# Output tiles of a routed feed-forward kernel: ScalarE copies both halves of a PSUM bank, and an accumulating transfer in SBUF adds them, in place of a VectorE add

## The chip, the cores and the metric

The kernel runs on one NeuronCore of a Trainium2 chip. The core has a matrix engine (TensorE, PE in the profile, with its weight loads as PEld), VectorE (DVE), ScalarE (ACT), GpSimd (POOL) and SyncE (SP), each with its own in-order instruction queue, and 16 DMA engines that they share. The metric is the device time of one execution in microseconds (us); lower is better.

## What is computed

```python
# x: 8 x 3584 x 192, weight: 8 x 7
w = softmax(weight, axis=-1)
attn[b, s, h] = sum_k w[h, k] * x_padded[b, s + k, h]      # causal 7-tap filter, 8 groups of 24 channels
x = attn.reshape(28672, 192)
logits = x @ w_gate                                        # 28672 x 8
# greedy by falling logit: a token goes to the expert of its best pair that still has room (3584 each)
for e in range(8):
    h = np.maximum(x[assigned == e] @ w1[e], 0)            # 192 -> 1024
    out[assigned == e] = h @ w2[e]                         # 1024 -> 192
```

All numbers are float32. The kernel reaches this precision with pairs of operands, a high part and a low part (the remainder), for weights and activations.

## The kernel before, in words

There are three kinds of work, and they overlap. The filter runs first and writes `attn` to HBM. The routing then finds, for every token, its expert: `half(0)`, `half(1)`, `rest` and `last` are generators, and one `next` of such a generator emits a few instructions, most of them for VectorE, some for ScalarE, and small matrix products into PSUM banks named `bg`. In `rest` stand `rounds` (thresholds for each expert; its tiles have names with `r_`, such as `r_w`, `r_x`, `r_v`) and then the building of index lists, in which VectorE makes one-hot tiles `oa`, TensorE multiplies them and ScalarE copies the products to `X`.

The feed-forward work is cut into 56 tiles of 512 tokens, and `run` goes over them. Tokens whose place is known early come first: eight tiles of one expert each, then pairs, and the tiles that need the end of the routing last. In iteration i of `run` a tile i is in its first layer (`l1`: eight steps f, five matrix products each into a bank `ph`; ScalarE makes the rectified high part `hh`, VectorE the remainder `hl`), tile i - 1 is in its second layer (`l2`: for each of its four blocks of 128 tokens 16 products into a bank `y`, two steps f per block), tile i + 1 gets its transposed input (`prep`), and for tile i + 2 GpSimd issues four gathers of token rows from HBM (`xg`).

A bank `y` holds 2 x 192 columns: columns 0 to 191 are the sum of two products, columns 192 to 383 a third, and the output is the sum of the two halves. `store` is called after each block, at the odd steps f. There ScalarE copies the second half to `yt`, and VectorE adds the first half from PSUM and `yt` to `yo`. `scatter` is called at the even steps; it pops the block and GpSimd issues an indirect transfer of the 128 rows of `yo` to their places in `out`. The pool `fo` has three buffers of `yo` and two of `yt`.

While the routing runs, the input is transposed by TensorE (`transp`: four products into `px` for channels 0 to 127, four more for the rest) and evacuated by ScalarE (`xa<-px`, `xd<-px`) and VectorE. Once no generator is left, `free()` holds, and the tile that is gathered then goes another way (`shuffle`: 16 pairs of VectorE block transposes into `xs`, no TensorE work).

What is put where in the engines' queues is decided while the program is written out. `Pace` adds up rough costs for every instruction (an estimate of its own, in `Meter`) for TensorE, VectorE and ScalarE, and `hook`, which is called in each step of `l1`, `l2` and `run`, emits the next piece of routing as long as VectorE's sum is no further than 1.8 us ahead of TensorE's. A piece that needs a result of VectorE or ScalarE is held back until TensorE's sum is past the producer's:

```python
v = self.need
if type(v) is tuple and self.route.cols < v[1] or type(v) is float and v > p.pe or p.dve > p.pe + slack or p.act > p.pe + act:
    return
self.run()
```

So an instruction less for VectorE in a block also moves the routing, and all that follows it, to earlier places in the program.

Of the kernel before, what the change touches and what calls it, by code (L numbers as in the profile page):

```python
# [6 lines left out]
F32 = mybir.dt.float32  # L7
# [3 lines left out]
AF = mybir.ActivationFunctionType  # L11
OP = mybir.AluOpType
# [3 lines left out]
NE, D, NTOK, F, CAP = 8, 192, 28672, 1024, 3584  # L16
# [12 lines left out]
class Meter:  # L29


    def __init__(self, pace, name, eng):
        self.pace, self.name, self.eng = pace, name, eng
# [1099 lines left out]
class FFN:  # L1133
# [3 lines left out]
    def __init__(self, tc, nc, attn, w1, w2, out, ident, wr, drm):  # L1137
        self.tc, self.nc = tc, nc

        self.kept1 = [drm.tile([128, 3, F], F32, name="kw%d" % e) for e in range(NE)]  # L1140
        self.keptd = [drm.tile([64, F], F32, name="kd%d" % e) for e in range(NE)]
        self.kept2 = [drm.tile([128, 8, 2 * D], F32, name="kv%d" % e) for e in range(NE)]
        self.attn, self.w1, self.w2, self.out, self.ident, self.wr = attn, w1, w2, out, ident, wr
        self.bg = lambda: None
        self.busy = lambda: False
        self.WT, self.RAW, self.XG, self.XT, self.H, self.Y, self.XS = {}, {}, {}, {}, {}, {}, {}
        self.wpa, self.wpb, self.DL = [None, None], [None, None], [None, None]
        self.scat, self.late = [], []
        self.free = set()
        self.xg = None  # L1150

# [163 lines left out]
    def store(self, i, b, idx):  # L1315
        nc = self.nc
        y = self.Y.pop((i, b))
        t = self.op.tile([128, D], F32, name="yt", bufs=2)
        o = self.op.tile([128, D], F32, name="yo")
        nc.scalar.activation(t, y[:, D:2 * D], AF.Copy)  # L1320
        nc.vector.tensor_tensor(o, y[:, 0:D], t, op=OP.add)
        self.late.append((o, idx))

    def scatter(self):

        if not self.late:
            return
        o, idx = self.late.pop()
        st = self.nc.gpsimd.indirect_dma_start(  # L1329
            out=self.out, out_offset=bass.IndirectOffsetOnAxis(ap=idx, axis=0), in_=o, in_offset=None,  # L1330
            bounds_check=NTOK - 1, oob_is_err=False)
        for s in self.scat:
            self.tc.declare_no_dep(st.ins, s.ins, reason="rows of other tokens")
        self.scat.append(st)
# [77 lines left out]
def moe_kernel(ctx, tc, x, weight, wg, w1, w2, out):  # L1412
    nc = Pace(tc.nc)
# [5 lines left out]
    with ExitStack() as cw:  # L1419
# [8 lines left out]
        r = Route(tc, nc, LT, lst, wk, drm)  # L1428
        r.oh_pool = oh
        r.bg = lambda: bgp.tile([128, 512], F32, name="bg")  # L1430
        ff = FFN(tc, nc, attn, w1, w2, out, r.ident, wr, drm)
# [21 lines left out]
        def half(h):  # L1453
            if h == 0:
                yield from r.thresh(0.905)
            yield from r.settle(h)
            yield from r.count(r.F, h)
            if h:
                yield from r.counts(NE)
            yield from r.lists(r.F, TA, h, 0 if h else None, *((ia, ja) if h else (ia0, ja0, 8, 4)),  # L1460
                               between=r.open() if h else None)

        def rest():
            yield from r.rounds()
            yield from r.final(NL)
            yield from r.lists(r.F, TB, 1, None, ib0, jb0, NL, 4, between=front())
# [5 lines left out]
        def last():  # L1472
            yield from r.sort4(0, TB, 1)
            yield from r.gather(TB, False)
            yield from r.tokens(TB, ib, jb)

        def tail():

            for i in (14, 15):
                for u in range(3):  # L1480
                    gate(i, u)
                    yield PEA if u == 2 else None
                end(i)
            nc.sync.dma_start(r.ltab, LT)
            c1.close()
            cs.close()
            ff.wpool2(cw, 1)
            ff.hp[1] = pool(cw, "fh1", 1, **late)
            yield

        bg = Steps(nc, r, (half(0), tail(), half(1), rest(), last()))
# [96 lines left out]
        ff.py = pool(cw, "py", 2, space=PSUM, **late)  # L1588
        ff.wpool2(cw, 0)
        ff.op = pool(cw, "fo", 3, **late)  # L1590
        ff.xp = pool(cw, "fp", 1, **late)
        ff.hp = [pool(cw, "fh0", 1, **late), None]
        ff.wpool(cw, 1)
# [60 lines left out]
```

## Time and profile before

| what | value |
|---|---|
| time before, median of 3 runs | 1268.94 us (1267.08 to 1273.11) |
| the profiled execution, its own time | 1281.97 us |
| its span, first to last instruction | 1280.2 us |
| TensorE busy, share of the span | 96% |
| VectorE busy | 78% |
| ScalarE busy | 43% |
| GpSimd busy | 40% |
| mean granted TensorE clock | 0.991 |

Busy shares are means over the whole span. TensorE's matrix products overlap one another and their ends are modelled, so a busy TensorE may still lose time; what counts is which wait ends last at a given place. In the rows below an instruction is named by its output, an arrow and its inputs; nearly all of them carry line L55, the helper that records them. An entry in square brackets is the idle time of the engine just ahead of the instruction, with the instruction that ended it.

### The profile page before, as it was taken

What the parts mean: (1) busy time and instruction counts of PE and PEld (TensorE: products, weight loads), DVE (VectorE), ACT (ScalarE), POOL (GpSimd) and SP (SyncE); (2) the same over time, 40 slices, a digit from 0 to 9 for tenths busy, and PEclk for the clock granted to TensorE, in tenths of its full rate; (3) what the DMA queues carried; (4) which work ended last, traced back from release to release, by engine and by line L of the source; (5) the groups of instructions that cost most, each with busy time, mean ns of one, the idle gap of its engine ahead of it and who ended that gap; (6) DMA issues with size and microseconds to landing.
All of it is one profiled execution on the core that took longest, in us unless ns stands there. A gap on an engine that the chain in (4) does not pass through costs nothing.

```text
span 1280.2 us, 21799 instructions
## 1 busy us (share of the span) xinstructions
PE 1228.3 (96%) x7847; PEld 1052.5 (82%) x7847; DVE 993.3 (78%) x2229; ACT 549.8 (43%) x1220; POOL 511.5 (40%) x504
## 2 busy tenths in 40 slices
PE   5989979999999999999989999999999999999997
PEld 2445558889889888888779999999999999999997
DVE  7398569799889999888866777777777777777772
ACT  4544645856444434443433333333333333333332
POOL 3000425355354444434144444444444444444422
PEclk9999989999999999999999999999999999999999
DMA  9999797999533343424453423232413232231100
GB/s 238 348 331 302 250 325 261 278 301 318 200 104 105 129 141 102 150 79 149 123 140 101 154 83 105 96 110 78 153 47 109 80 104 97 65 123 47 47 23 30
DMA packets 100579, 193.02 MB, mean 151 GB/s; under 512 B 19232, under 2 KB 64752, under 8 KB 96240
## 3 DMA queue, kind: packets, MB, share of 16 engines
q1 hardware_dynamic: 57856, 115.15, 27.5%
q0 software_dynamic: 21504, 44.07, 11.7%
q10 hardware_dynamic: 21104, 32.34, 7.7%
q8 instruction: 63, 1.03, 0.3%
q14 instruction: 52, 0.43, 0.1%
HBM read 116.02 MB, written 75.50 MB: 150 GB/s over the span
## 4 chain that ended last, share of the span: by engine, by line
PE 86%; DMA 5%; DVE 5%; ACT 2%; issue 1%; SPq 1%; another core or an unknown queue 0%; POOL 0%; POOLq 0%; ACTq 0%; DVEq 0%
PE ph L55 38%; PE y L55 38%; PE cv L55 4%; DMA X<-in_x_dram 3%; PE bg L55 3%; DMA raw<-in_moe_w_dram 2%; PE px L55 1%; PE pl L55 1%; DVE aT L55 1%; DVE X L55 1%; DVE oa L55 1%; ACT a_d L55 1%; DVE hl L55 0%; DMA kd<-dl 0%
## 5 line engine op out<-in xcount | busy, mean ns | idle before, releaser
L55 PE MATMUL y<-w,hh 128*128 128x384 f32 x1792 | 541.6, 358 | 0.0
L55 ACT ACTIVATE hh<-ph 128x512 fp32r<-128x512 f32 x448 | 267.9, 598 | 493.9 <-PE ph L55 457.9
L55 PE MATMUL y<-w,hl 128*128 128x192 f32 x1792 | 449.9, 251 | 0.0
L55 DVE SCALAR_TENSOR_TENSOR hl<-ph,hh 128x512 fp32r<-128x512 f32 x448 | 308.2, 688 | 144.4 <-ACT hh L55 121.4
L55 PE MATMUL ph<-xa,w 128*128 128x512 f32 x1344 | 395.1, 402 | 1.2 <-DVE hl L55 1.1
L55 PEld LDWEIGHTS y<-w,hl 128*128 128x128 f32 x1792 | 342.2, 191 | 15.0
L55 PEld LDWEIGHTS y<-w,hh 128*128 128x128 f32 x1792 | 337.5, 188 | 18.6 <-issue 1.9
L1329 POOL DMA_INDIRECT out_dram<-yo,ib x128 | 128.2, 1001 | 288.2 <-DVE yo L55 278.0
L55 PEld LDWEIGHTS ph<-xa,w 128*128 128x128 f32 x1344 | 218.9, 189 | 21.7 <-DVE hl L55 2.6
L1329 POOL DMA_INDIRECT out_dram<-yo,ia x96 | 111.7, 1164 | 268.5 <-DVE yo L55 237.2
L55 DVE STREAM_TRANSPOSE xs<-xg 32x256 f32<-32x256 f32 x480 | 176.8, 368 | 8.2
L55 PE MATMUL ph<-xd,w 128*128 128x512 f32 x448 | 177.5, 396 | 1.1 <-DVE xd L55 1.1
L55 PE MATMUL ph<-xd,dl 128*128 128x512 f32 x448 | 174.6, 390 | 0.4 <-DVE dl L55 0.4
L1254 POOL DMA_INDIRECT xg<-attn,jb x128 | 139.0, 1086 | 44.9 <-issue 40.6
L1254 POOL DMA_INDIRECT xg<-attn,ja x96 | 110.7, 1153 | 33.3 <-issue 26.2
L55 ACT ACTIVATE yt<-y 128x192 f32<-128x192 f32 x224 | 73.5, 328 | 114.3 <-PE y L55 91.2
L55 PE MATMUL cv<-X,TH 118*128 118x384 f32 x256 | 101.7, 522 | 17.3 <-DVE TH L55 12.4
L55 DVE TENSOR_TENSOR yo<-y,yt 128x192 f32<-128x192 f32 x224 | 79.6, 355 | 42.4 <-ACT yt L55 39.2
L55 PEld LDWEIGHTS ph<-xd,w 128*128 128x128 f32 x448 | 84.1, 188 | 21.1 <-DVE xd L55 1.6
L55 PEld LDWEIGHTS ph<-xd,dl 128*128 128x128 f32 x448 | 84.3, 188 | 20.3 <-DVE dl L55 0.7
L55 PEld LDWEIGHTS cv<-X,TH 118*128 118x128 f32 x256 | 45.0, 197 | 51.0 <-issue 14.5
L55 ACT ACTIVATE a<-cv 128x384 f32<-128x384 f32 x128 | 59.9, 492 | 57.2 <-PE cv L55 40.5
(237 smaller groups left out, 904.4 us busy)
## 6 DMA issues: line engine op xcount, KB each, us to landing
w<-kw SPq DMA_DIRECT2D x16, 1536.0 KB
w<-kv SPq DMA_DIRECT2D x16, 1536.0 KB
attn<-a ACTq DMA_DIRECT2D x16, 1344.0 KB
kw<-w SPq DMA_DIRECT2D x48, 256.0 KB
kv<-w SPq DMA_DIRECT2D x32, 384.0 KB
X<-in_x_dram SPq DMA_DIRECT2D x17, 672.0 KB
X<-in_x_dram ACTq DMA_DIRECT2D x15, 672.0 KB
raw<-in_moe_w_dram SPq DMA_DIRECT2D x32, 192.0 KB
```

Source lines behind the costliest of these rows:

```text
L55: return f(*a, **k)
L1254: self.nc.gpsimd.indirect_dma_start(out=t[:, b], out_offset=None, in_=self.attn[0:rows], in_offset=bass.IndirectOffsetOnAxis(ap=idx[b], ax ...
L1329: st = self.nc.gpsimd.indirect_dma_start(out=self.out, out_offset=bass.IndirectOffsetOnAxis(ap=idx, axis=0), in_=o, in_offset=None, bounds ...
```

## The change

From the eighth tile on (`i > 6`) and as long as routing generators are left, `store` gives VectorE nothing. ScalarE copies all 384 columns of the bank to a tile `yo` that now has two halves. At the next even step `scatter` issues, from GpSimd, a transfer inside SBUF that adds the second half onto the first (`accum_op=OP.add`), and one even step later the indirect transfer of the first half to `out`. In the other tiles ScalarE's copy goes into the second half of the same tile, and VectorE adds as before. The pool `fo` has three such tiles.

```diff
@@ class FFN
-        t = self.op.tile([128, D], F32, name="yt", bufs=2)
-        o = self.op.tile([128, D], F32, name="yo")
-        nc.scalar.activation(t, y[:, D:2 * D], AF.Copy)
-        nc.vector.tensor_tensor(o, y[:, 0:D], t, op=OP.add)
-        self.late.append((o, idx))
+        o = self.op.tile([128, 2, D], F32, name="yo")
+        if self.bydma(i):
+
+            nc.scalar.activation(o.rearrange("p h d -> p (h d)"), y[:, 0:2 * D], AF.Copy)
+            self.sums.append((o, idx))
+            return
+        nc.scalar.activation(o[:, 1], y[:, D:2 * D], AF.Copy)
+        nc.vector.tensor_tensor(o[:, 0], y[:, 0:D], o[:, 1], op=OP.add)
+        self.late.append((o[:, 0], idx))
 
     def scatter(self):
 
-        if not self.late:
-            return
-        o, idx = self.late.pop()
+        ready, self.late = self.late, []
+        if self.sums:
+            o, idx = self.sums.pop()
+            self.nc.gpsimd.dma_start(o[:, 0], o[:, 1], accum_op=OP.add)
+            self.late.append((o[:, 0], idx))
+        for r in ready:
+            self.rows(*r)
+
+    def rows(self, o, idx):
         st = self.nc.gpsimd.indirect_dma_start(
             out=self.out, out_offset=bass.IndirectOffsetOnAxis(ap=idx, axis=0), in_=o, in_offset=None,
             bounds_check=NTOK - 1, oob_is_err=False)
@@ moe_kernel
+        ff.bydma = lambda i: bg.gens and i > 6
```

In the whole program 60 of the 224 blocks take the new way. The emitted programs differ further in this: 25 tiles are transposed by TensorE, where before there were 26, and 31 go by `shuffle`, where there were 30.

On GpSimd's queue, about the tenth tile, the program before has this (`xg<-attn` are the gathers, `out_dram<-yo` the indirect transfers to the output; `x4` stands for four in a row):

```order
L1254 DMA xg<-attn,ja 128x192 x4
L1329 DMA out_dram<-yo,ia 28672x192 x4
L1254 DMA xg<-attn,ja 128x192 x4
L1329 DMA out_dram<-yo,ia 28672x192 x4
L1254 DMA xg<-attn,ja 128x192 x4
```

The changed program has this for one tile (`yo<-yo` are the accumulating transfers):

```order
L1255 DMA xg<-attn,ja 128x192 x4
L1334 DMA yo<-yo 128x192
L1340 DMA out_dram<-yo,ia 28672x192
L1334 DMA yo<-yo 128x192
L1340 DMA out_dram<-yo,ia 28672x192
L1334 DMA yo<-yo 128x192
L1340 DMA out_dram<-yo,ia 28672x192
L1334 DMA yo<-yo 128x192
L1340 DMA out_dram<-yo,ia 28672x192
```

A tile has twelve transfers on this queue in place of eight, and each transfer to the output stands behind the accumulating transfer of the next block.

On VectorE's queue the third of four places in `rounds` where a result `r_v` goes back to TensorE reads as follows before (the two `r_x` that read `bg` are the first to use the products of that round):

```order
L55 MAX r_w<-X_6386 128x8 x2
L55 SCALAR_TENSOR_TENSOR hl<-ph,hh 128x512
L55 TENSOR_TENSOR yo<-y,yt 128x192
L55 SCALAR_TENSOR_TENSOR r_x<-bg,room 128x8
L55 SCALAR_TENSOR_TENSOR r_x_3179<-bg,room_2148 8x1
L55 TENSOR_SCALAR r_x<-r_x 128x8
L55 TENSOR_SCALAR r_x_3179<-r_x_3179 8x1
L55 TENSOR_SCALAR r_pen<-r_x_3179 8x1
L55 TENSOR_SCALAR r_x_3179<-r_x_3179 8x1
L55 MAX r_s_6704<-bg 8x8
```

The same place in the changed program:

```order
L55 MAX r_w<-X_6273 128x8 x4
L55 SCALAR_TENSOR_TENSOR hl<-ph,hh 128x512
L55 TENSOR_TENSOR xd<-px,xd 64x512
L55 SCALAR_TENSOR_TENSOR hl<-ph,hh 128x512
L55 SCALAR_TENSOR_TENSOR r_x<-bg,room 128x8
L55 SCALAR_TENSOR_TENSOR r_x_3166<-bg,room_2147 8x1
L55 TENSOR_SCALAR r_x<-r_x 128x8
L55 TENSOR_SCALAR r_x_3166<-r_x_3166 8x1
L55 TENSOR_SCALAR r_pen<-r_x_3166 8x1
L55 TENSOR_SCALAR r_x_3166<-r_x_3166 8x1
```

No add of an output block stands ahead of the round's first reader any more; a remainder `hl` does. On TensorE's queue the same round's `r_v` product now has 8 first-layer and 12 second-layer products between it and the round's `r_w` transposes, where before there were 8 and 8. The place itself moved from 147 whole first-layer steps into the program to 144, and the routing's last product from the sixth step of tile 24 to the first.

## Rows read from the trace of the kernel before

**Rows 1.** The profile's page: busy us and share of each engine, instructions.

```profile
PE 1228.3 (96%) x7847; PEld 1052.5 (82%) x7847; DVE 993.3 (78%) x2229; ACT 549.8 (43%) x1220; POOL 511.5 (40%) x504
```

**Rows 2.** Stretches: length, busy us by engine, granted clock, DMA share, GB/s.

```profile
230.00:360.00 130.00, 127.48 (x755) 113.95 (x754) 114.74 (x265) 77.58 (x193) 64.66 (x54) 1.00 0.81 262
...
340.00:520.00 180.00, 179.00 (x1053) 160.12 (x1052) 163.46 (x406) 77.94 (x191) 81.58 (x72) 1.00 0.36 119
520.00:560.00 40.00, 38.09 (x216) 34.16 (x216) 34.24 (x77) 18.58 (x51) 14.89 (x15) 0.96 0.30 88
560.00:640.00 80.00, 78.17 (x597) 67.79 (x596) 68.60 (x166) 31.71 (x68) 24.58 (x24) 1.00 0.42 131
640.00:680.00 40.00, 36.54 (x316) 31.46 (x316) 27.10 (x61) 14.98 (x29) 19.24 (x18) 0.96 0.45 121
```

**Rows 3.** Waits of TensorE from 340 to 700 us: us, times, longest.

```profile
PE bg L55 <- ACT X L55: 2.2, 3, 0.9
PE bg L55 <- DVE r_v L55: 1.9, 1, 1.9
PE bg L55 <- DVE hl L55: 1.7, 1, 1.7
```

**Rows 4.** Timeline, 537 to 546 us: start us, us, engine, instruction.

```profile
541.17 0.33 ACT L55 ACTIVATE yt<-y 128x192 f32<-128x192 f32 x1 [2.39 <-PE ph L55]
...
541.54 0.36 DVE L55 TENSOR_TENSOR yo<-y,yt 128x192 f32<-128x192 f32 x1 [2.03 <-ACT yt L55]
541.81 0.21 DVE L55 SCALAR_TENSOR_TENSOR r_x<-bg,room 128x8 f32<-128x8 f32 x2
...
543.64 0.26 DVE L55 TENSOR_SCALAR r_v<-r_v,r_pen 8x1 f32<-8x1 f32 x1
...
543.96 0.22 PE L55 MATMUL bg<-ident,r_v 8*128 8x8 f32 x1 [1.91 <-DVE r_v L55]
```

**Rows 5.** The two stretches of 5 us about that place.

```profile
540.00:545.00 5.00, 3.09 (x15) 2.46 (x15) 3.29 (x14) 1.31 (x3) 1.01 (x1) 0.91 0.23 63
545.00:550.00 5.00, 5.00 (x26) 4.62 (x26) 4.93 (x14) 1.53 (x3) 0.98 (x1) 0.75 0.01 3
```

**Rows 6.** Timeline of TensorE, two first-layer steps about 444 us.

```profile
443.02 0.88 PE L55 MATMUL ph<-xa,w 128*128 128x512 f32 x3
...
444.19 0.60 PE L55 MATMUL px<-ident,xg 128*64 128x128 f32 x4
...
445.75 0.88 PE L55 MATMUL ph<-xa,w 128*128 128x512 f32 x3
...
448.04 0.88 PE L55 MATMUL ph<-xa,w 128*128 128x512 f32 x3
```

**Rows 7.** The page's groups: busy us, mean ns, idle before.

```profile
L55 ACT ACTIVATE hh<-ph 128x512 fp32r<-128x512 f32 x448 | 267.9, 598 | 493.9 <-PE ph L55 457.9
L55 DVE SCALAR_TENSOR_TENSOR hl<-ph,hh 128x512 fp32r<-128x512 f32 x448 | 308.2, 688 | 144.4 <-ACT hh L55 121.4
...
L55 DVE STREAM_TRANSPOSE xs<-xg 32x256 f32<-32x256 f32 x480 | 176.8, 368 | 8.2
L55 ACT ACTIVATE yt<-y 128x192 f32<-128x192 f32 x224 | 73.5, 328 | 114.3 <-PE y L55 91.2
L55 DVE TENSOR_TENSOR yo<-y,yt 128x192 f32<-128x192 f32 x224 | 79.6, 355 | 42.4 <-ACT yt L55 39.2
L55 ACT ACTIVATE a<-cv 128x384 f32<-128x384 f32 x128 | 59.9, 492 | 57.2 <-PE cv L55 40.5
```

**Rows 8.** Groups of GpSimd from 340 to 700 us, as in rows 7.

```profile
L1329 POOL DMA_INDIRECT out_dram<-yo,ia x67 | 72.6, 1084 | 187.3 <-DVE yo L55 162.0 <-DVE r_oki L55 5.5 <-DVE r_x L55 5.0
L1254 POOL DMA_INDIRECT xg<-attn,ja x52 | 58.4, 1123 | 15.9 <-issue 14.6 <-PE ph L55 0.6 <-PE bg L55 0.3
```

**Rows 9.** Instructions on `yo`: ns min/median/max, first and last start us.

```profile
L1329 POOL DMA_INDIRECT out_dram<-yo,ia x96: 981/1037/3728, 192.7 to 700.4; - x96
```

**Rows 10.** A piece of the chain that ended last: start us, us.

```profile
238.91 5.60 DMA raw<-in_moe_w_dram
```

More of the change, by code (lines that the diff above doesn't have):

```diff
@@ L1147, in __init__ @@
         self.wpa, self.wpb, self.DL = [None, None], [None, None], [None, None]
-        self.scat, self.late = [], []
+        self.scat, self.late, self.sums = [], [], []
+        self.bydma = lambda i: False
         self.free = set()
```

## The prediction

> **What bounds the kernel now.** I read the page first: of a span of 1280.2 us TensorE is busy 96%, VectorE 78% [rows 1]. A mean of that kind says little, so I went to the stretches. The change acts from about 315 us (eighth tile) to about 700 us. From 340 to 520 us TensorE is idle for 1.0 us of 180 and VectorE is busy 163.5 us, 91% [rows 2]. VectorE is nearly full there, yet TensorE hardly ever waits for it: the queues are written so that VectorE is fed as much routing as fits under TensorE. The reader is to see that relief of VectorE in this stretch is not time; it is room that the program fills with routing.
>
> What TensorE does lose lies in a few places. From 520 to 680 us it is idle 1.9, 1.8 and 3.5 us in the three stretches [rows 2], so with the 1.0 us before that 8.2 us in all, and the waits that have a name are few: one of 1.9 us for `r_v`, one of 1.7 us for `hl`, three for `X`, 2.2 us together [rows 3]. Two of the stretches also show a mean granted clock of 0.96 [rows 2]. The first belongs to the `r_v` wait: after 1.9 us idle the granted clock goes to 0.91 and 0.75 in the next two stretches of 5 us [rows 5], that is part of them at 1.2 GHz in place of 2.4, and costs (0.09 + 0.25) x 5 = 1.7 us. The second has the same mean over 40 us, 1.6 us. All that the routing's waits cost from 340 to 680 us is thus 8.2 + 3.3 = 11.5 us, and no removal of VectorE work can bring more than this, except by TensorE work that disappears.
>
> **Why TensorE waits for r_v.** This is the place that matters most [rows 4]. VectorE is done with all before at 541.54 - 2.03 = 539.5 us and then does nothing for 2.03 us, because the next in its queue is the add of an output block, which waits for ScalarE's `yt`, and this starts at 541.17, when TensorE has ended the bank `y`. The round's first reader `r_x` stands behind this add and starts at 541.81, `r_v` ends at 543.9, TensorE goes on at 543.96. The chain from `r_x` to `r_v` takes 543.90 - 541.81 = 2.1 us. Had it begun when VectorE was free, at 539.5, it would have ended at 541.6, before TensorE's earliest need at 543.96 - 1.91 = 542.05.
>
> **The change, part by part.** VectorE loses 60 adds of 355 ns [rows 7], 21.3 us, and gains one tile's `shuffle`, 16 transposes of 368 ns, 5.9 us. Its stretch is covered by TensorE either way, so this counts nothing directly; what it does is bring the routing's last product forward by five steps.
>
> TensorE: because the routing ends earlier, one tile more goes by `shuffle`. A step with four `px` takes 445.75 - 443.02 = 2.73 us, the next without 2.29 [rows 6]. Two such groups in a tile are 2 x 0.44 = 0.9 us, saved once: **-0.9 us**. The other products are the same in number.
>
> The `r_v` wait: in the changed program no add stands ahead of `r_x`; the last instruction ahead is an `hl` whose bank `ph` is full before the `r_w` products. The chain of 2.1 us then runs beside 8 first-layer and 12 second-layer products. Five first-layer products take 444.19 - 443.02 = 1.17 us, and the eight second-layer ones the rest of a 2.29 us step, 1.12 [rows 6]; so these take 8 x 0.234 + 12 x 0.14 = 3.55 us. That leaves 1.4 us, enough for another `hl` of 0.69 [rows 7] or a late ScalarE. I take the wait as gone, with its clock: 1.9 + 1.7 = **-3.6 us**. The other end is that it stays, 0. The other three `r_v` places had no wait (the row counts one [rows 3]) and have no add in front any more either.
>
> ScalarE: a copy of 384 columns takes 492 ns where it reads a bank in the filter [rows 7], one of 192 takes 328, so each block costs 164 ns more, 9.8 us in all. ScalarE is busy 77.9 of 180 us there [rows 2]; it waits for the bank before most copies [rows 7], and what stands behind is an `hh`, whose remainder is needed a tile later. Bounds: nothing, or 0.16 us at each of the three places where TensorE waits for ScalarE's `X` [rows 3], +0.5 us. I take nothing, as nearly always `hh` alone is delayed.
>
> The add was also the last reader of a bank `y`. Now ScalarE alone frees it, 0.49 us after the last product in place of 0.33 + 0.36 [rows 7]. No wait of TensorE for it is in the list, so this is nothing.
>
> GpSimd: 60 accumulating transfers. The trace has no direct transfer on this queue and none that adds, so I bound the issue from below by the shortest indirect one, 0.98 us, from above by the longest, 3.73 us [rows 9]. I take 1.08 us, the mean of those to `out` in the stretch [rows 8], since it too has 128 rows of 768 bytes. With 0.3 us between two (14.6 us over 52, [rows 8]) a tile needs 4 x 1.38 + 4 x 1.42 = 11.2 us before, and 11.2 + 5.5 = 16.7 us after. A tile takes 8 x 2.29 + 0.9 = 19.2 us [rows 6]. It fits, at 87%.
>
> The landing: no row shows how long such a transfer takes to land. The block's transfer to `out` is issued two steps, 4.6 us, after. From above it is bounded by a load of weights on the chain, 5.6 us [rows 10], from below by nothing. At 5.6 us GpSimd would wait 1.0 us per block, four per tile, and need 20.7 us a tile, 1.5 too many, +22 us over 15 tiles. I take under 4.6 us and so nothing, because that load ran in a stretch with DMA engines 81% busy, and from 340 us on they are 30 to 45% busy [rows 2]. By the Trainium skill's "DMA: Bandwidth & Descriptors", section on the anatomy of one DMA on the gpsimd path, a transfer costs about 2.0 us plus its bytes at 436 GB/s, an estimate of 2.2 us for these 98 KB; no run here shows it, and the sum by it would be the same.
>
> The buffers: ScalarE's copy of a block now waits until the output transfer of the third block before it has landed; that block's own copy was six steps of 2.29, 13.7 us, earlier. Latest is the one behind the gathers: after its own copy (0.5) come its accumulate and an older output transfer (2 x 1.38), four gathers (5.7) and one more accumulate (1.38), so it is issued at about 10.4 us and has 3.3 us to land. If it takes longer, the copy and the `hh` behind it are late once per tile. TensorE has three banks `ph`: a bank is needed again two steps after it is full, and `hh` and `hl` take 0.60 + 0.69 us [rows 7], so up to 2 x 2.29 - 1.29 = 3.3 us more are covered. I take nothing.
>
> The sum is -0.9 - 3.6 = -4.5 us of the profiled 1280.2 us span (1281.97 with what lies around it). The median of the runs shown is 13 us lower, all tiles alike, so I put the same 4.5 us on it: 1268.9 - 4.5 = **1264.4 us**.
>
> **The rivals.** (a) *The wait is only moved*: the emission shifts everywhere, and some other piece of routing is now read too early. One wait like the `r_v` one costs 3.6 us. Then -0.9 - 3.6 + 3.6 gives 1268.0; with two, 1271.6. For it: at 640 to 680 us TensorE loses 3.5 us where lists are built, with waits for ScalarE's `X` and `hl` [rows 2, 3], which no add removes. Against: VectorE has more room than the emission counts on, since a real add took 355 ns and its share is gone altogether.
>
> (b) *All of the waits shrink*: a VectorE queue without adds that wait for a bank is never blocked by TensorE's own pace, and the list building loses its waits too. The bound is -0.9 - 11.5, that is 1256.5; half of the rest gives 1260.5. Against: the largest sum among the waits is that for ScalarE's `X` [rows 3].
>
> (c) *GpSimd becomes the bound* (the other side). If an accumulating transfer holds the queue for more than (19.2 - 11.2) / 4 - 0.3 = 1.7 us, tiles outrun it; the three buffers fill, ScalarE's copy blocks with `hh` behind it, and TensorE follows. At 2.2 us a tile needs 21.2 us, 2.0 more over 15 tiles: +30 us, 1294. At 3.73 us it would be 27.3 us a tile, near 1386. For it: one transfer did take 3.73 us. Against: that one lies outside the stretch, whose means are 1.08 and 1.12 us with VectorE at 91% [rows 2, 8]. The Trainium skill's "SBUF — State Buffer", section on a bandwidth-pool intuition, says that GpSimd cannot write descriptors while VectorE runs an operation that takes both ports, and gives 620 ns alone against about 3100 ns. By that figure all blocks would be in this case; by the rows of this stretch, with the same VectorE work beside the issues, hardly any is.
>
> **How the numbers follow.** The forecast, about 1261 to 1267 us, has a chance of 0.50; (a) 0.24; (b) 0.21; (c) 0.05. Within 0.5% of 1268.9 means 1262.6 to 1275.3, about what a measurement of this kernel tells from no change. Faster: (b) and a fifth of the forecast's own spread, 0.31. Slower: (c) and a little of (a), 0.07. Same: 0.62. The range goes from the middle of (b) to the far end of (a): 1258.5 to 1271.6 us; what it leaves out is (c) and the lower half of (b), under 0.2.
>
> **What would show it.** Right: TensorE's wait for `r_v` near 530 us is gone and the granted clock stays at 1.00 there; the 25th tile has no `px`; tiles without routing products still take 19.2 and then 18.3 us; ScalarE's copies take about 0.49 us; the accumulating issues about 1.1 us, and GpSimd still has idle time between blocks. Wrong: waits of 1.5 us and more elsewhere between 340 and 680 us, with a fall of the clock after them; or ScalarE's copy released by GpSimd or a DMA; or a tile period above 20 us through the whole stretch.

## The result, and the profile after

The changed kernel takes 1275.9 us (median of 13 runs, 1271.9 to 1279.9), the kernel before beside it 1270.01 us (13 runs). The medians are 5.9 us apart; the ratio that the runs give is 1.004, interval 1.0029 to 1.0051, which is 5.1 us. So the change makes the kernel slower by 0.4%, and the interval excludes 1, where 4.5 us less was forecast. The profiled execution took 1273.04 us, its span is 1271.2.

The page of the changed kernel, its busy line, which answers to [rows 1]: TensorE has 7839 products in place of 7847, the eight `px` of one tile.

```profile
PE 1220.1 (96%) x7839; PEld 1047.9 (82%) x7839; DVE 983.1 (77%) x2185; ACT 559.6 (44%) x1220; POOL 569.4 (45%) x564
```

The stretches of [rows 2], in the changed kernel (us, PE, PEld, DVE, ACT, POOL busy, granted clock, DMA share, GB/s). TensorE idles 0.01, 0, 2.0 and 0 us, and the clock is 1.00 in all four.

```profile
340.00:520.00 180.00, 179.99 (x1062) 160.59 (x1061) 159.11 (x375) 87.01 (x207) 116.70 (x108) 1.00 0.50 136
520.00:560.00 40.00, 40.00 (x240) 35.72 (x238) 34.83 (x88) 19.07 (x45) 24.77 (x24) 1.00 0.52 145
560.00:640.00 80.00, 77.99 (x690) 66.74 (x689) 66.32 (x143) 34.73 (x65) 40.13 (x38) 1.00 0.58 150
640.00:680.00 40.00, 40.00 (x246) 36.24 (x245) 25.52 (x61) 15.26 (x30) 19.76 (x20) 1.00 0.38 93
```

Its waits of TensorE from 311 to 700 us, against [rows 3]: `r_v`, `hl` and `X` are gone.

```profile
PE bg L55 <- DVE c_bi L55: 1.1, 2, 0.7
PE bg L55 <- DVE u_b L55: 0.7, 1, 0.7
PE bg L55 <- DVE F L55: 0.2, 1, 0.2
```

Its instructions on `yo` (ns min/median/max, first and last start us), against [rows 9], and the time from issue to landing of the accumulating transfers alone, which the trace has for 26 of the 60:

```profile
L55 ACT ACTIVATE yo<-y x224: 309/332/494, 189.6 to 1258.7; 128x192 f32<-128x192 f32 x82, 128x384 f32<-128x384 f32 x30
L1340 POOL DMA_INDIRECT out_dram<-yo,ia x96: 982/1056/3739, 190.6 to 686.2; - x96
L1334 POOL DMA_DIRECT2D yo<-yo x60: 887/907/1021, 336.5 to 648.2; - x60
...
DMA to landing us min/median/max: 2.5/2.6/5.1
```

Nearly all this is what the prediction wanted to see, and yet the kernel is slower. The end of the chain shows where the time is (start us, us, what): the last transfer's issue ends at 1260.68, and the span at 1271.2. Some 10.5 us follow in which no engine does anything that the views count as work.

```profile
core 0 of [0], span 1271.2 us
...
1259.06 0.36 DVE yo L55
...
1259.51 0.51 POOLq L1634
1260.02 0.66 POOL out_dram L1340
```

### The profile page after: what moved, and what is told of

Read it like the earlier page. It is cut to its first block, busy times and chain, and to the rows that moved or that the text cites. A ratio compares the mean times of both kernels' runs of the same rounds, so it can differ in the third digit from the quotient of the medians.

```text
span 1271.2 us, 21868 instructions
## 1 busy us (share of the span) xinstructions
PE 1220.1 (96%) x7839; PEld 1047.9 (82%) x7839; DVE 983.1 (77%) x2185; ACT 559.6 (44%) x1220; POOL 569.4 (45%) x564
## 4 chain that ended last, share of the span: by engine, by line
PE 84%; DVE 6%; DMA 5%; issue 1%; ACT 1%; POOL 1%; SPq 1%; POOLq 0%; ACTq 0%; DVEq 0%
PE ph L55 38%; PE y L55 37%; PE cv L55 3%; PE bg L55 3%; DMA raw<-in_moe_w_dram 2%; DVE X L55 1%; DMA X<-in_x_dram 1%; PE px L55 1%; DMA wgr<-in_moe_w_gate_dram 1%; DVE aT L55 1%; DVE hl L55 1%; PE pl L55 1%; DVE oa L55 1%; POOL xg L1255 0%; DVE sl L55 0%
## 5 line engine op out<-in xcount | busy, mean ns | idle before, releaser
L55 DVE STREAM_TRANSPOSE xs<-xg 32x256 f32<-32x256 f32 x496 | 182.9, 369 | 8.5
L1340 POOL DMA_INDIRECT out_dram<-yo,ia x96 | 114.9, 1197 | 120.3 <-DVE yo L55 82.7
L55 ACT ACTIVATE yo<-y 128x192 f32<-128x192 f32 (+1 forms) x224 | 83.2, 371 | 107.1 <-PE y L55 101.6
L1334 POOL DMA_DIRECT2D yo<-yo x60 | 56.2, 937 | 77.0 <-ACT yo L55 70.1
L55 DVE TENSOR_TENSOR yo<-y,yo 128x192 f32<-128x192 f32 x164 | 58.3, 355 | 35.6 <-ACT yo L55 33.5
```

The costliest lines, as they stand in the source:

```text
L55: return f(*a, **k)
L1334: self.nc.gpsimd.dma_start(o[:, 0], o[:, 1], accum_op=OP.add)
L1340: st = self.nc.gpsimd.indirect_dma_start(out=self.out, out_offset=bass.IndirectOffsetOnAxis(ap=idx, axis=0), in_=o, in_offset=None, bounds ...
```

## Two questions

The traces raise two questions. Did the stretch gain what [rows 3, 4] promise? And what is in the last 10 us? To compare kernels I read two lengths from each trace: the **stretch**, from the first product of the eighth tile's first layer to that of the 26th, in which alone the change acts, and the **tail**, from the end of VectorE's last addition to the end of the span.

My theory was: the profiled execution of before was not like the runs that it is compared with, its waits are absent in them, so the stretch has little to give; and the tail is what the change costs, since GpSimd's longer program and its new transfers lengthen what GpSimd does after its last transfer. The rivals: the wider `yo` tile costs something; or the stretch itself became worse.

## The experiments: the stretch

**The kernel before, once more** (no edit).

> The kernel before, unchanged, profiled once more. Its earlier profiled execution took 1281.97 us where its other runs have a median of 1270; the changed kernel's profiled execution took 1273.0 where its median is 1275.9. Theory T (the loss is at the program's end): the wait for r_v of 1.9 us near tile 19, on which the prediction rested, is no fixed part of the kernel; here the span is near 1268 us, the tiles 8 to 24 take about 352 to 355 us together as in the changed kernel (353.7), and from the last add of an output block to the end of the span it takes 6.8 us again (12.1 in the changed kernel). Rival S (the stretch): the r_v wait is there again and the tail varies by itself between 6 and 12 us.

Measured: 1267.96 us, span 1266.2. The same program, and its waits of TensorE from 311 to 700 us are these, with none for `r_v` or `hl`:

```profile
PE bg L55 <- ACT X L55: 1.3, 2, 0.7
PE bg L55 <- DVE u_b L55: 0.6, 1, 0.6
PE bg L55 <- DVE r_cc L55: 0.2, 1, 0.2
```

At the place of [rows 4] its timeline reads:

```profile
531.88 0.60 ACT L55 ACTIVATE hh<-ph 128x512 fp32r<-128x512 f32 x1 [1.70 <-PE ph L55]
...
533.26 0.30 PE L55 MATMUL bg<-r_c,onesf 128*128 128x8 f32 x2
533.46 0.33 ACT L55 ACTIVATE yt<-y 128x192 f32<-128x192 f32 x1 [0.98 <-PE y L55]
...
534.10 0.21 DVE L55 SCALAR_TENSOR_TENSOR r_x<-bg,room 128x8 f32<-128x8 f32 x2
...
535.93 0.26 DVE L55 TENSOR_SCALAR r_v<-r_v,r_pen 8x1 f32<-8x1 f32 x1
...
537.15 0.22 PE L55 MATMUL bg<-ident,r_v 8*128 8x8 f32 x1
```

The bank `y` is full just ahead of the product of `r_c`, and ScalarE's `yt` starts 0.2 us after that product's start. `r_v` ends at 536.19, 0.96 us before TensorE comes to it. Span by span, the changed kernel against this one: start of the eighth tile +0.1 us, stretch 372.6 to 372.0 us (-0.6), later tiles the same, tail 6.27 to 11.83 us (+5.6); in all +5.1, as the times of these two executions differ, 1273.04 and 1267.96 us. The end of this chain:

```profile
core 0 of [0], span 1266.2 us
...
1259.55 0.36 DVE yo L55
...
1260.00 0.51 POOLq L1622
1260.52 0.66 POOL out_dram L1329
```

**The tile layout alone.**

```diff
-        ff.bydma = lambda i: bg.gens and i > 6
+        ff.bydma = lambda i: False
```

> The changed kernel with the new way switched off for all tiles (the two-half tile in the pool fo stays, all blocks are added by VectorE): it computes the same. Theory T: the instruction counts of before are back, so the tail is 6.8 us and the time that of before, ratio 0.999 to 1.001. Rival L (the larger pool moves later buffers and brings new waits at the start): slower than before by 2 to 5 us, ratio 1.002 to 1.004.

Measured: 1269.31 us, ratio 0.9995 (0.9982 to 1.0008), stretch 372.8, tail 6.23. On this chip, of the first kind named below, the wider tile costs nothing that the runs can tell.

**The changed kernel and the kernel before, again and again** (no edits), because in a later comparison the kernel before took about 1280 us. That happened on other chips: medians of 1269.2 to 1270.3 on some, of 1279.9 to 1281.8 on others. I call them the first and the second kind. Each comparison met another chip, so that whether the chip or the occasion makes the kind is not shown.

> The changed kernel as it is, once more, beside the kernel before. So far the kernel before took about 1270 us in two comparisons and about 1280 in a third, on another chip, where kernels with its order of work needed 380 us from the eighth tile to the start of the 26th in place of 372.6, with the wait for r_v in them. D (what the change brings in that stretch depends on whether ScalarE is late there, which differs from chip to chip; its end costs 5.5 us on any): where the kernel before takes about 1270, the ratio is 1.003 to 1.005 as before; where it takes about 1280, the stretch is 372 to 374 us and the ratio 0.997 to 1.000. S (the ratio is the kernel's own and chips only scale it): 1.003 to 1.005 on either.

> The kernel before, profiled once more beside the others, to see its stretch on this chip. D: where the kernel before takes about 1270 in this comparison, 372.6 us and no wait for r_v near the tile 18 (20.4 us); where it takes about 1280, about 380 us and tile 18 at 22 us or more. S: 372.6 to 373 us times the ratio of the chips' medians, with no single tile that stands out.

> The changed kernel as it is, a third time, to meet a chip on which the kernel before takes about 1280 us. D: there its stretch from the eighth tile to the start of the 26th is 372 to 374 us, tile 18 about 19.2, and the ratio 0.997 to 1.000; on a chip where the kernel before takes about 1270 the ratio is 1.003 to 1.005 again. S: 1.003 to 1.005 on any.

> The kernel before, profiled on the same chip. D: its stretch is 380 us where it takes about 1280 (tile 18 at 22 us or more), 372.5 where it takes about 1270. S: no tile stands out on any chip.

Measured: e9 and e12 met a chip of the first kind (before 1269.16): ratio 1.0041 (1.0025 to 1.0057), stretches 372.0 (after) and 372.4 (before). e13 and e14 met one of the second (before 1281.84): ratio 1.0019 (1.0004 to 1.0033), stretches 376.7 (after) and 383.7 (before). So D holds for the stretch in its direction and S falls: on a chip of the second kind the kernel before has the wait, and the change removes it. In size D is off: 376.7 us lies above its 372 to 374. Waits of TensorE from 311 to 700 us, e14 (before):

```profile
PE bg L55 <- DVE hl L55: 1.9, 1, 1.9
PE bg L55 <- DVE r_v L55: 1.9, 1, 1.9
PE bg L55 <- ACT X L55: 1.3, 2, 0.7
```

and the same place in its timeline:

```profile
537.41 0.30 PE L55 MATMUL bg<-r_c,onesf 128*128 128x8 f32 x2
...
538.89 0.60 ACT L55 ACTIVATE hh<-ph 128x512 fp32r<-128x512 f32 x1 [4.55 <-PE bg L55]
...
540.50 0.33 ACT L55 ACTIVATE yt<-y 128x192 f32<-128x192 f32 x1 [1.01 <-PE ph L55]
...
541.14 0.21 DVE L55 SCALAR_TENSOR_TENSOR r_x<-bg,room 128x8 f32<-128x8 f32 x2
...
543.29 0.22 PE L55 MATMUL bg<-ident,r_v 8*128 8x8 f32 x1 [1.91 <-DVE r_v L55]
```

Measured from the product of `r_c`, ScalarE's `hh` starts 1.38 us earlier in e1 and 1.48 us later in e14: 2.86 us late. With the 0.96 us that `r_v` had to spare, 1.9 us are left, and that is the wait. TensorE had filled that `ph` in time; nothing in the trace holds ScalarE. In this trace and in the first one of before ScalarE is late at the same instructions of the program, some 15 of them after 300 us, mostly by 1.2 to 1.5 us, five of them in the even run of tiles after 750 us; in e1 and e12 at none. One of the five, first in the profile of before, then in e1:

```profile
794.07 0.33 ACT L55 ACTIVATE yt<-y 128x192 f32<-128x192 f32 x1 [1.70 <-PE ph L55]
```

```profile
779.03 0.33 ACT L55 ACTIVATE yt<-y 128x192 f32<-128x192 f32 x1 [0.52 <-PE y L55]
```

The changed kernel has no wait for `r_v` there either way (e13, 311 to 700 us):

```profile
PE bg L55 <- DVE c_bi L55: 2.6, 2, 2.2
PE px L55 <- DVE xa L55: 0.7, 1, 0.7
```

The ratio of e13 is above D's 0.997 to 1.000. The stretch gave 7.0 us and the tail took 5.2, which is -1.8, and 2.4 us more were measured. In the two profiles the eighth tile starts at 318.8 and 313.1 us, 5.7 us apart, ahead of all accumulating transfers; single profiles on such chips scatter from 312.8 to 318.8 there. What makes the rest of 4.2 us is open. A rival stands: on the chip of e13 and e14 the two kernels with the wider tile (e13, e16) start it at 318.8 and 317.1, the two without (e14, e15) at 313.1 and 313.9, and e9 and e10 are 1.4 to 2.5 us later than e11 and e12 on theirs. On e5's chip no such difference is seen, and the wide tile alone (e2) ran on a chip of the first kind only.

**The order alone.** VectorE adds as before, but the routing is emitted as if it did not.

```diff
-            nc.scalar.activation(o.rearrange("p h d -> p (h d)"), y[:, 0:2 * D], AF.Copy)
-            self.sums.append((o, idx))
+            nc.scalar.eng.activation(o[:, 1], y[:, D:2 * D], AF.Copy)
+            nc.act = max(nc.act, nc.pe) + 0.12 + 2 * D / 1400
+            nc.vector.eng.tensor_tensor(o[:, 0], y[:, 0:D], o[:, 1], op=OP.add)
+            self.late.append((o[:, 0], idx))
```

> The changed kernel's order of work alone: the routing is emitted as in the changed kernel (the sums that pace it are kept as if no addition were made), but ScalarE copies one half and VectorE adds the halves as before, so there is no accumulating transfer. O (the order is what helps, VectorE has the room): stretch from the eighth tile to the start of the 26th 372 to 373.5 us, tail 6.3 us, tile 25 without px; where the kernel before takes 1270 the ratio is 0.998 to 1.000, where it takes 1280 it is 0.993 to 0.996. R (the additions must be gone as well, since VectorE is overfilled otherwise): stretch 375 us or more with new waits of TensorE for VectorE, ratio 1.000 to 1.006.

Measured, first kind: 1273.35 us, ratio 1.0027 (1.0014 to 1.004), stretch 375.2, tail 6.47. R holds, O falls. In the stretch the order without the relief loses 2.8 us against e12, and with the relief (e9) it is 3.2 us shorter again. TensorE's waits from 311 to 690 us are the changed kernel's, two of them longer, and one for `r_cc`:

```profile
PE bg L55 <- DVE c_bi L55: 1.7, 2, 1.0
PE bg L55 <- DVE F L55: 1.0, 1, 1.0
PE bg L55 <- DVE r_cc L55: 0.7, 3, 0.3
PE bg L55 <- DVE u_b L55: 0.7, 1, 0.7
```

**The addition one step later.** In the same tiles VectorE's addition is emitted in `scatter`, a step after ScalarE's copy.

```diff
     def store(self, i, b, idx):
-        nc.vector.tensor_tensor(o, y[:, 0:D], t, op=OP.add)
+        if self.later(i):
+            self.adds.append((o, y, t))
+        else:
+            nc.vector.tensor_tensor(o, y[:, 0:D], t, op=OP.add)
...
     def scatter(self):
         o, idx = self.late.pop()
+        if self.adds:
+            o, y, t = self.adds.pop()
+            self.nc.vector.tensor_tensor(o, y[:, 0:D], t, op=OP.add)
...
+        ff.later = lambda i: bg.gens and i > 6
```

> The kernel before, with VectorE's addition of a block emitted one step later in the same tiles (from the eighth on, while routing is left), so that ScalarE's copy is long done when VectorE comes to it; no transfer is added. If a VectorE that stands before an addition for ScalarE's copy is what holds the routing, the waits of the stretch go without a price at the program's end: tail 6.3 us, stretch 371.5 to 373 us on any chip, ratio 0.998 to 1.000 where the kernel before takes 1270, 0.993 to 0.996 where it takes 1280. If it is the shifted order that costs (as in e10), stretch 374 to 376 us, ratio 1.001 to 1.003 where the kernel before takes 1270.

> The kernel of e15 (VectorE's addition one step later) once more, for a chip on which the kernel before takes about 1270 us. There no routing result is waited for in that kernel, so that the saving of e15 should be gone: stretch 371.5 to 374.5 us, tail 6.3 us, ratio 0.999 to 1.002. Where the kernel before takes about 1280, 0.995 to 0.999 again.

> The kernel of e15 a third time, as e17, which met a chip on which the kernel before takes 1280 us. Where the kernel before takes about 1270: stretch 371.5 to 374.5 us, tail 6.3 us, ratio 0.999 to 1.002. Where it takes about 1280: 0.995 to 0.999 again.

Measured: e15 on the second kind 1278.86 us against 1281.84, ratio 0.997 (0.9954 to 0.9986), stretch 378.6; e17 on the second kind 0.9976 (0.9964 to 0.9988), stretch 377.4; e18 on the first kind 1268.12 us against 1270.34, 0.998 (0.9968 to 0.9992), stretch 370.8. Tails 6.37 to 6.63. This version beats the kernel before on either kind, and the changed kernel too. On the first kind it gains more than expected; on the second e15 gains less (0.993 to 0.996 and a stretch of 371.5 to 373 were expected, "on any chip"). There TensorE has other waits in place of the one for `r_v`, in e15 1.5 us for `r_cc`, 1.4 for `c_bi` and 1.2 for a bank `y` that the later addition frees later. In e15 ScalarE is late as in e14 (idle 4.70 us with no work for it to wait for), but the round's readers are already done:

```profile
539.01 0.22 DVE L55 SCALAR_TENSOR_TENSOR r_x<-bg,room 128x8 f32<-128x8 f32 x2
...
541.36 0.26 DVE L55 TENSOR_SCALAR r_v<-r_v,r_pen 8x1 f32<-8x1 f32 x1
...
542.28 0.22 PE L55 MATMUL bg<-ident,r_v 8*128 8x8 f32 x1
543.06 0.33 ACT L55 ACTIVATE yt<-y 128x192 f32<-128x192 f32 x1 [4.70 <-PE bg L55]
```

## The experiments: the tail

Once the last transfer is issued, GpSimd's queue holds in each kernel a conditional branch over the general path, two waits for semaphores, a semaphore instruction for its transfers (INC_SWDGE_SEM) and a drain. They are in the trace's records, not in the views of busy time:

```
kernel                 transfers      gap after    INC_SWDGE_SEM  drain   tail
                       in SBUF        branch, us   ns             ns      us
e1  before             0              0.43          652           3414     6.27
e12 before             0              0.43          652           3609     6.46
e4  before + 73 memsets 0             3.72          652           2039     8.20
e6  before + 4 plain   4              0.44          760           3548     6.50
e7  before + 8 plain   8              0.44          842           3672     6.72
e16 after, half        31             0.44         1614           5791     9.64
e5  after, ninth on    56             0.44         1272           5317     8.81
e11 before + 56 plain  56             0.44         1784           6612    10.62
    after              60             3.65         1400           4974    11.83
e9  after              60             4.06         1400           4974    12.24
e3  after + 55 memsets 60             0.44         1400           5114     8.75
e8  after, seventh on  64             0.44         1512           5423     9.16
```

**Idle memsets, to move the program's end.** A memset of one column on GpSimd behind each of the last transfers, 55 in the changed kernel (e3), 73 in the kernel before (e4).

```diff
...
         self.scat.append(st)
+        if len(self.scat) > 120 and self.pads:
+            self.pads -= 1
+            self.nc.gpsimd.memset(self.pad, 0.0)
...
```

> The changed kernel with 55 GpSimd memsets of a 128 x 1 scratch tile, one behind each output transfer late in the program where GpSimd is idle. They bring GpSimd's instruction count at the last branch from 1318 to 1373, which is 128 more than the 1245 of before; instructions are fetched in pieces of 8192 bytes, which would be 128 of them. Theory T: the 3.7 us in which GpSimd has no instruction after the branch go, the tail falls from 12.1 to about 7 us, and the time falls by about 5 us to 1270 to 1271, ratio to before near 1.000. Rival S (the accumulating transfers and the wider copies cost in the stretch): no change against the changed kernel, ratio 1.004 to 1.005.

> The kernel before with 73 of the same memsets, which bring GpSimd's instruction count at the last branch to 1318, that of the changed kernel. Theory T: the tail grows to about 12 us and the time by about 5 us, ratio 1.003 to 1.005, with nothing else changed. Rival S: 73 memsets in idle time of GpSimd cost nothing, ratio 0.999 to 1.001.

Measured, first kind: e3 1271.85 us, ratio 1.0012 (0.9997 to 1.0027), tail 8.75; e4 1271.17 us, ratio 1.0009 (0.9996 to 1.0023), tail 8.20. The gap comes and goes with the memsets as T says, but T's sizes fail: e3's tail is 8.75 us and not about 7, e4's 8.20 and not about 12, and e4's ratio stays below T's 1.003 to 1.005. In these runs the gap behind the branch goes with the program's length alone: counted in the trace the branch is GpSimd's instruction 1318 in the changed kernel and in e4, which have it, and 1245, 1373 or another in those that don't. The trace's DMA records also hold the loads of instructions, 8192 bytes each on queue q14. Behind the branch there are six in each of the four executions with GpSimd's gap and five in those without; the one exception, e16 with six, has a gap of 3.45 us on ScalarE instead. So in the gap GpSimd most likely waits for instructions that have to be loaded. In e4 the later drain is 1.4 us shorter, so part of it is a wait that runs beside the gap. Of the 5.6 us the gap is 3.2; the other 2.3 are the last two instructions, (1.40 + 4.97) - (0.65 + 3.41).

**Other counts and kinds of transfers.** e5 and e8 start the new way at the ninth and the seventh tile (`i > 7`, `i > 5`, with 60 and 50 memsets); e6 and e7 add plain transfers to the kernel before, and e11 56 of them with as many memsets; in e16 only every second block goes the new way (`if b % 2 == 0 and self.bydma(i)`).

```diff
...
         self.scat.append(st)
+        if len(self.scat) > 120 and self.pads:
+            self.pads -= 1
+            self.nc.gpsimd.dma_start(self.pad[:, 0:128], self.pad[:, 128:256])
...
```

> The changed kernel with accumulating transfers from the ninth tile of the routing on instead of the eighth (56 of them, so 504 transfers issued by GpSimd, a multiple of eight, instead of 508), and 60 idle memsets on GpSimd in the late tiles so that its program ends where e3's did, without the fetch gap of 3.7 us. P (GpSimd's last semaphore instruction and its drain are long because the number of its transfers is not a multiple of the eight semaphores that they rotate over): the semaphore instruction is back at about 650 ns and the drain at about 3.4 us, the tail behind the last addition at about 6.3 us, the time 1268.5 to 1270, 0.999 to 1.000 of the kernel before. K (they are long because of transfers between places of SBUF at all) and C (because of accumulating ones): 1400 ns and about 5.1 us as in e3, tail 8.7, time about 1271.8. Stretch from the eighth tile to the start of the 26th: 372.0 to 373 for all.

> The kernel before, with four plain transfers of 128 x 128 values from one place of SBUF to another added on GpSimd's queue in the late tiles (452 transfers, not a multiple of eight); their data is not used. P: the semaphore instruction 1400 ns and the drain about 5 us, the tail about 8.5 us. K: the same. C: 650 ns and 3.4 us, tail 6.3 us. The single time can tell little; the profile decides.

> As e6 with eight such transfers (456, a multiple of eight). P: 650 ns and about 3.4 us, tail 6.3 us. K: 1400 ns and about 5 us, tail 8.5 us. C: 650 ns, 3.4 us, tail 6.3 us.

> The changed kernel with accumulating transfers from the seventh tile on (64 of them, 512 transfers of GpSimd, a multiple of eight) and 50 idle memsets. P: 650 ns and about 3.4 us, tail 6.3 us, time 1268 to 1270. K and C: 1400 ns and 5.1 us, tail 8.7 us, time 1271 to 1272.5. The seventh tile's pieces may go earlier too, by up to 1 us.

> The kernel before with 56 plain transfers of 128 x 128 values inside SBUF on GpSimd's queue in the late tiles, whose data is not used, and 56 idle memsets so that the program's end lies where no fetch gap was seen. N (GpSimd's last semaphore instruction and drain grow with the number of direct transfers on its queue, whether they add or not): 1270 ns and about 5.3 us as with 56 accumulating ones in e5, tail 8.5 to 9 us. A (adding is what costs): not above e7's, 840 ns and 3.7 us, tail below 7 us.

> The changed kernel with every second block by the new way, about 30 accumulating transfers. N: GpSimd's last semaphore instruction and drain lie between those with eight and with 56 (840 to 1270 ns, 3.7 to 5.3 us), about 1050 ns and 4.5 us, less where a fetch gap stands ahead of them; the stretch between 372 and 375 us.

Measured: the table. P falls: e5 and e8, multiples of eight, have 1272 and 1512 ns. C falls with the 760 and 842 ns of plain transfers in e6 and e7, and K's 1400 ns are not reached there. A falls too: 56 plain transfers cost 1784 ns and 6.6 us, more than accumulating ones, though they also stand later in the program and are smaller. N is right that any transfer inside SBUF on GpSimd's queue makes its end longer, by 0.1 us of semaphore instruction for four, but wrong that the number sets it: 31 in e16 cost more than 56 to 64. What sets it is open. e5, e6, e7, e8 and e16 ran on the second kind: e5 1276.22 us, 0.9978 (0.9959 to 0.9996) with the stretch at 372.5 and without the gap; e8 0.9999 (0.9983 to 1.0015), stretch 374.6; one run each of e6, e7 and e16, of 1283.19, 1282.88 and 1280.01 us, with stretches of 380.2, 379.6 (the order of the kernel before) and 374.4; e11's one run, on the first kind, 1273.92.

## Why the prediction was wrong

**The step that failed** is the last of the sum: "all tiles alike, so I put the same 4.5 us on it". The profiled execution was not longer in all tiles alike. Against e1 its span is 14.0 us longer, and of these 10.3 lie in the stretch: 3.5 in the 19th tile, where the priced wait for `r_v` stands (23.9 against 20.4 us), and 5.5 in the 22nd to 24th. On a chip of the first kind, such as the comparison ran on, the term of -3.6 us for `r_v` has nothing to remove, and the stretch gave 0.6 us in place of 4.5.

**Why `yt` was late** was misread. "This starts at 541.17, when TensorE has ended the bank `y`": the row's own releaser is a product into `ph`, and the bank `y` had been full for some 3 us, as e14's rows against e1's show; ScalarE was late without a cause in the trace. The wait that VectorE showed was true, the releaser behind it was not looked at. On a chip of the second kind the mechanism is as told: e13's stretch is 7.0 us shorter than e14's, and in e15 the wait for `r_v` is gone without the transfers.

**What was left out** is the end of the program. No term and no rival had it, and its 5.6 us are more than the whole of what was forecast; the slower side came from there and not from (c). The median lies 11.5 us above the forecast: 5.6 of them are the tail, 3.9 the stretch, 1.1 the median of before, which is 1270.0 in these runs; 0.9 is not accounted for. The tail alone would have given 1270.0 us and the stretch alone 1268.3, both inside the range.

**What was right.** The `px` term: the tile that loses its `px` takes 18.29 us in place of 19.21, -0.9; the other tiles move by up to 3.6 us either way and together give 0.3 of it back. ScalarE's copies take up to 494 ns and cost TensorE nothing; its own waits for a landing, one of the signs of being wrong, are 2.3 us in all, 3 times, and TensorE did not wait for them. The accumulating issue takes 907 ns, less than the 1.08 taken, and GpSimd does not become the bound. The landing takes 2.6 us at the median, inside the 4.6; four of the 26 that the trace has take 4.9 to 5.1, and GpSimd waited for a landing 7 times, 10.5 us in all. The Trainium skill's "DMA: Bandwidth & Descriptors", section on the anatomy of one DMA on the gpsimd path, gives an estimate of 2.2 us; the trace has 2.5 as its shortest. The Trainium skill's "SBUF — State Buffer", section on a bandwidth-pool intuition, gives about 3100 ns, in place of 620, for a transfer issued by GpSimd beside a VectorE copy that holds the port they share. None of the 60 issues took over 1021 ns, and no run here shows whether VectorE's operations hold that port.

**"Relief of VectorE is not time; it is room"** fits e10: in the stretch filling the room costs 2.8 us, the relief returns 3.2. Rival (a) described that half, a routing that is read too early.

## What to carry to other kernels

When the profiled execution stands 1% from the runs that the metric is taken from, first find in which tiles it is longer: if that is where the priced waits are, they may not exist in the runs, and a second profile is worth more than a finer sum. An instruction that waits for another engine and isn't urgent is better placed a step later than handed to a transfer: that took one edit and gained 0.2 to 0.3% on either kind of chip. New transfers on GpSimd's queue also have a price once per program, behind the last useful work, and the chain of the page ends before it.

## What was not expected of the hardware

ScalarE was late at the same instructions of the same program in two executions, by 1.2 to 2.9 us (one on the second kind, the other the first profile of before, whose chip is not recorded), and at none of them in two on the first kind; the kernel takes 10 us longer there. GpSimd's branch at the end took 0.43 us to the next instruction or 3.5 to 4.1 us, by the program's length alone in these runs and with one more load of instructions in the second case (VectorE's takes 3.5 to 4.2 us in all of them, while GpSimd's queue is still at work). GpSimd's last drain takes 3.4 to 3.8 us (2.0 behind the gap of e4), with transfers inside SBUF up to 6.6, and exactly 4974 ns in all three profiled executions of the changed kernel.
